# Moving five indirect DMAs in GpSimd's queue of a fused top-k attention and mixture-of-experts kernel

## The chip, the cores and the metric

The kernel runs on one core of one Trainium2 chip. The metric is device time in microseconds (us) of one execution, the median of several runs. In the profile PE is TensorE's matmuls, PEld its weight loads, DVE is VectorE, ACT is ScalarE, POOL is GpSimd and SP is SyncE, which only issues DMAs here.

## The reference, cut to what matters

```python
# attention: 8 batches, 8 heads, 576 tokens, head size 64, top_k = 32
scores = scale * np.matmul(q, k.transpose(0, 1, 3, 2))
kth = np.partition(scores, -top_k, axis=-1)[..., -top_k:-top_k + 1]
scores = np.where(scores >= kth, scores, -1000000000.0)
attn = softmax(scores)
x = np.matmul(attn, v)        # then (B,H,S,D) -> (B*S, H*D) = (4608, 512)
# experts: 8 of them, 512 -> 1024 -> 512, one for each token
logits = x @ w_gate
expert_idx = np.argmax(logits, axis=1)
gate_w = softmax(logits)[np.arange(N), expert_idx]
for e in range(E):            # the rows of expert e, no row dropped
    h = np.maximum(x_sorted[lo:hi] @ w1[e], 0.0)
    y_sorted[lo:hi] = h @ w2[e]
out = gate_w[:, None] * y
```

Everything is float32. The 32nd largest score of each row has to be found exactly, and each attention row goes to one expert.

## The kernel before, in words

**Tiling.** A unit is a pair of heads of one batch, so there are 8 x 4 = 32 units. The attention runs in 144 slots, the passes of the loop at L1250 over `work` (18 slots in a batch, 9 for two units; NT is 9 and NC is 4). A slot handles two tiles of 128 query rows by 576 keys.

**One slot.** TensorE computes the scores three slots ahead (L304), ACT copies them to SBUF (L311), and DVE folds each row's 576 scores into pairwise maxima `h` and minima `l` (`fold`, L320 and L321) and once more (`fold_on`, L327, and L335 or, in some slots, two integer operations on GpSimd, L332 and L333). `search` (L358) then finds the top 32 by four rounds of MAX8 and MATCH_REPLACE8 on DVE (L379, L390). The folds of the next slot ride inside the search of this one: with `soon` after its second round, otherwise ahead of its last, and L320 and L321 come behind it. From the 32nd value ACT makes `low` (L401) and, with a steep ReLU, a mask (`depths`, L417). GpSimd subtracts that from the scores (`less`, L426, two operations), ACT takes the exponential (L434), TensorE transposes the weights (L445, L461), and multiplies them with the values (L482).

**GpSimd's queue in a slot** holds, in order: `nbias` (L385, behind the search's first round of maxima; the exponentials need it), sometimes L332 and L333, the two `less` (L426), `doubts` (L407), and then the indirect DMAs that `put_stores` and `scatter` issue. Every fourth or fifth slot is one "with a unit's rows beside it": the search's callback `beside` (L1271) puts the unit's gate logits (L519 to L524) and its rows (`rows`, L533, a 128x640 multiplication into the tile `x`) right behind `nbias`. Before slot 66 (QUIET) these are the slots whose number leaves 3 or 8 on division by 9. Such a slot is called a rows slot below.

**Scatters and stores.** When a batch's four units are through, its rows go to the experts' places in the DRAM tensor `x_rows`, in five indirect DMAs (L601), one in each slot from number 6 of the next batch on (`scatter(1)`). In the first 66 slots these are slots 24 to 28, 42 to 46 and 60 to 64. After a batch's last scatter its full blocks of 128 rows become work: SP loads their weights and rows, TensorE computes them in pieces between the attention's matmuls (L979, L996), ACT scales the result into `y` (L1005), and the indirect DMA of L888 stores it in the output. The block leaves its store in the list `stores`, and `put_stores` issues it at the end of the next slot's GpSimd work, or from within a block (`following`).

**What sets the order.** The program writes out the order of PE, ACT and DVE by hand (`manual_schedule`), and `in_turn` and `add_manual_dep` keep GpSimd's in the order of the program. `k.crowded` is set by every scatter, store and `rows`; a crowded slot is not `soon` and keeps L335 on DVE instead of L332 and L333 on GpSimd. After slot 143, the remaining expert blocks run on TensorE to the end.

Of the kernel before, what the change touches and what calls it, by code (L numbers as in the profile page):

```python
# [44 lines left out]
def kernel(  # L45
# [54 lines left out]
    NC = 4  # L100
# [7 lines left out]
    NT = 2 * NC + 1  # L108
# [25 lines left out]
    k = SimpleNamespace()  # L134
# [172 lines left out]
    def scores(got):  # L307

        s = k.att.tile([P, 2, 2, HF], F32, name="s", bufs=2 if k.exact else 4)
        return s, [  # L310
            lambda m=m, ps=ps: nc.scalar.copy(s[:, m, :, :], ps[:, :, 0:HF]) for m, ps in enumerate(got)  # L311
        ]

    def fold(s, parts=(slice(0, 2),)):

        f = SimpleNamespace()
        f.h = k.att.tile([P, 2, HF], F32, name="h", bufs=1)
        f.l = k.att.tile([P, 2, HF], F32, name="l")
        for m in parts:
            nc.vector.tensor_tensor(f.h[:, m], s[:, m, 0, :], s[:, m, 1, :], op=ALU.max)  # L320
            nc.vector.tensor_tensor(f.l[:, m], s[:, m, 0, :], s[:, m, 1, :], op=ALU.min)  # L321
        return f
# [696 lines left out]
    QUIET = 66  # L1019
# [4 lines left out]
    with fast:  # L1024
# [8 lines left out]
        per_batch = len(work) // B  # L1033
        x_of, lg_of = {}, {}
        waiting, loaded, coming, spare, scatters, stores = [], [], [], [], [], []
        current = None
        left = clock = 0

        def level(b):

            have, sums = left / PIECES, []
            for n, new in enumerate(new_of[b:] + [0], 1):
                sums.append(have / n)
                have += new
            sums[-1] = (have - KEEP / PIECES) / (len(sums) - 1 + (per_batch - FIRST) / per_batch)
            return min(sums)
# [4 lines left out]
        def ahead():  # L1051
            while waiting and len(loaded) < 2:
                expert, piece = waiting.pop(0)
                if isinstance(piece, SimpleNamespace):
                    rows_in = piece
                elif isinstance(piece, list):
                    rows_in = load_half(load_rows(SimpleNamespace(), piece[0]), *piece[1:])
                elif isinstance(piece, tuple):
                    rows_in = load_rows(SimpleNamespace(), *piece, full=True)
                else:  # L1060
                    rows_in = load_rows(SimpleNamespace(), piece)
                loaded.append(load_weights(rows_in, expert))
                loaded[-1].at = clock

        def put_stores():
            while stores:
                k.crowded = True
                stores.pop(0)()

# [30 lines left out]
        def scatter(n):  # L1100
            nonlocal left
            for _ in range(min(n, len(scatters))):
                k.crowded = True
                scatters.pop(0)()
            if not scatters and coming:
                waiting.extend(coming)
                left += len(coming) * PIECES
                coming.clear()
                ahead()
# [99 lines left out]
        def at_place(name):  # L1209
            for end in list(late):  # L1210
                if end[1] == name:
                    end[1] = next(end[0], None)
                    if end[1] is None:
                        late.remove(end)
# [10 lines left out]
        def multiply(i):  # L1225
            tiles = tiles_of(i)
            got_of[i] = products(tiles, i < AHEAD)
            n, tile = tiles[0]
            more = n.b * U + n.u + 2
            if tile == (NC - 1 if n.u % 2 else 2 * NC) and more < len(units):  # L1230
                unit.append(load_unit(*units[more]))

        def loop():
            nonlocal credit, rate, clock
            for i in range(min(AHEAD, len(work))):
                multiply(i)
                s_of[i], steps = scores(got_of.pop(i))
                for step in steps:
                    step()
            multiply(AHEAD)  # L1240
            for step in prepared:
                step()
            for odd in range(2):
                for h in range(2):
                    r = slice(h * D, (h + 1) * D)
                    at = odd * (lw + P) + h * E
                    nc.vector.tensor_copy(turn[r, :, at:at + E], wg[r, odd::2, :])
            f_of[0] = fold(s_of[0], (slice(0, 1), slice(1, 2)))
            fold_on(f_of[0])
            for i, (b, g) in enumerate(work):  # L1250
                tiles = tiles_of(i)
                u, tile = g[0]
                if tile == 0 and u % 2 == 0:
                    open_unit(tiles[0][0])
                if tails(tiles):
                    open_unit(tiles[1][0])

                loose = 0 < i < QUIET
                k.heavy = loose and "rows" in [place for _, place in late]
                soon = loose and (k.heavy or not k.crowded)  # L1260
                then = behind = beside = lambda: None
                if i + 1 < len(work):
                    def behind():
                        f_of[i + 1] = fold(s_of[i + 1])

                    then = lambda: fold_on(f_of[i + 1], soon and not k.heavy)
                    if i:
                        behind()
                        behind = lambda: None
                if k.heavy:  # L1270
                    beside = lambda: at_place("rows")  # L1271
                held = k.heavy and k.crowded
                low, nbias, doubts = search(tiles, s_of[i], f_of.pop(i), then, soon, behind, beside)
                k.crowded, k.heavy = held, False
                at_place("small")
                w_of[i] = depths(s_of[i], low)
                less(s_of.pop(i), w_of[i])
                doubts()
                at_place("pool")
                if not loose:  # L1280
                    at_place("relu")
                    at_place("rows")
                put_stores()
                scatter(1)
                at = i % per_batch
                if at == FIRST and b:
                    rate = level(b) * PIECES / (U * NT)
                credit += rate * len(g)
                room = left
                if b == B - 1 and at >= ARRIVED:  # L1290
                    room -= KEEP
                    credit = room / (len(work) - i)
                share = {0: 0.5, 1: 1.2, 2: 1.6, 3: 0.5, 2 * NC: 1.4}[tile]
                now = max(0, min(int(credit * share + 0.5), room))
                credit -= now
                clock = i
                if i + AHEAD < len(work):
                    s_of[i + AHEAD], steps = scores(got_of.pop(i + AHEAD))
                    for step in steps:
                        step()  # L1300
                if loose:
                    at_place("relu")
                evacuate()
                at_place("turn")
                turns = turning(i - 1) if i else iter(())
                next(turns, None)
                part = min(BETWEEN, now - now // 2)
                rest = pieces(part)
                next(turns, None)
                rest = pieces(now - now // 2 - part + rest)  # L1310
                weights(tiles, w_of[i], nbias)
                next(turns, None)
                evacuate()
                if i + AHEAD + 1 < len(work):
                    multiply(i + AHEAD + 1)
                if tile == NC - 1:
                    end = ending(b, u)
                    late.append([end, next(end)])
                at_place("products")
                at_place("weights")  # L1320
                credit = min(credit + pieces(now // 2 + rest), 6 * rate)

            k.between = True
            for _ in turning(len(work) - 1):
                pieces(1)
            assert len(late) == 1
            clock = None
            for place in late[0][0]:
                if place == "rows":
                    pieces(4)  # L1330
            kept = left - (SURE + HALVES + PLAIN) * PIECES
            assert kept >= 0, kept
            k.apart = True
            pieces(kept)
# [139 lines left out]
```

## Time and profile before

| What | Value |
|---|---|
| Median of 3 runs (lowest to highest) | 1285.07 us (1283.54 to 1285.09) |
| The profiled execution: its own time | 1284.61 us |
| Its span, first to last instruction | 1283.0 us |
| Busy: PE, PEld | 1176.1 us, 823.6 us |
| Busy: DVE, ACT, POOL | 1058.8 us, 933.3 us, 732.0 us |
| L601, the scatter, on POOL | 40 times, 1065 ns mean |
| L888, the store, on POOL | 37 times, 1052 ns mean (and 4 of 908 ns) |
| L533, `rows`, on POOL | 32 times, 1411 ns mean, 1253 ns at least |
| L320 and L321, the folds on DVE | 145 times each, 770 and 788 ns mean |
| Granted TensorE clock | 0.967 of full speed |

A timeline gives, for each instruction, its start in us from the span's start, its duration in us, the engine, the line, the operation, what it writes and reads, how many were merged, and in brackets the idle time ahead of it with what ended that. An instruction that another engine holds up after it was started shows this as a longer duration, not as idle time.

### The profile page before, as it was taken

How to read it: one execution, taken by the hardware profiler on the slowest of the kernel's cores; microseconds unless marked ns; L12 is line 12 of the kernel's file. 1: busy time of each engine (PE TensorE's matmuls, PEld its weight loads, DVE VectorE, ACT ScalarE, POOL GpSimd, SP SyncE). 2: the span in 40 equal slices, each digit the busy share in tenths (PEclk: the TensorE clock that was granted, in tenths of full speed). 3: DMA queues.
4: the chain of work that ended last, by engine and by line, in shares of the span. 5: the costliest groups of instructions: out<-in, count | busy, mean ns of one | idle time of the engine just before them, and what ended most of it. 6: DMA issues, size and time to landing. Idle time of an engine off the chain costs nothing. (4 is left out here: it accounts for less than half of the span.)

```text
span 1283.0 us, 24461 instructions
## 1 busy us (share of the span) xinstructions
PE 1176.1 (92%) x7574; PEld 823.6 (64%) x7574; DVE 1058.8 (83%) x4608; ACT 933.3 (73%) x2136; POOL 732.0 (57%) x884
## 2 busy tenths in 40 slices
PE   6767767898899999999999999999999999999998
PEld 3444444665566566667666666666666667789975
DVE  8999999999999999999999999999999965000000
ACT  4888887988799888888788888888888872112121
POOL 4777777786678665658555855676557743101010
PEclk9888788999899999999999999999999999999999
DMA  5001113741474147533946464547555548996582
GB/s 153 31 30 31 31 39 126 263 157 39 146 251 162 39 150 283 182 135 98 332 142 218 163 224 153 189 146 264 178 178 202 172 149 285 353 358 235 215 301 83
DMA packets 98701, 220.81 MB, mean 172 GB/s; under 512 B 5309, under 2 KB 26301, under 8 KB 98560
## 3 DMA queue, kind: packets, MB, share of 16 engines
q1 hardware_dynamic: 91360, 198.87, 44.5%
q0 software_dynamic: 6384, 19.97, 4.2%
q8 instruction: 61, 1.00, 0.3%
q14 instruction: 80, 0.66, 0.2%
q10 hardware_dynamic: 816, 0.31, 0.1%
HBM read 195.75 MB, written 24.04 MB: 171 GB/s over the span
## 5 line engine op out<-in xcount | busy, mean ns | idle before, releaser
L426 POOL TENSOR_TENSOR w<-s,w 128x576 f32<-128x576 f32 x288 | 409.2, 1441 | 317.5 <-ACT w L417 317.4
L979 PE MATMUL ph<-xTs,w 128*128 128x128 f32 x2112 | 263.0, 278 | 2.6 <-ACT xTs L870 2.6
L979 PEld LDWEIGHTS ph<-xTs,w 128*128 128x128 f32 x2112 | 251.3, 194 | 21.1 <-issue 17.6
L996 PE MATMUL py<-w,hT 128*128 128x512 f32 x528 | 248.7, 600 | 1.9 <-ACT hT L984 1.6
L434 ACT ACTIVATE w<-w,nbias 128x576 f32<-128x576 f32 x288 | 223.0, 785 | 2.3 <-POOL w L426 1.4
L445 PE MATMUL wTm<-turn,w 128*128 128x128 f32 x1152 | 173.9, 291 | 52.7 <-ACT oT L484 29.1
L417 ACT ACTIVATE w<-s,low 128x576 f32<-128x576 f32 x288 | 207.7, 768 | 4.7
L304 PE MATMUL sc<-qkb 64*128 64x288 f32 (+1 forms) x1280 | 200.7, 465 | 7.8 <-DMA qkb<-in_qk_dram 4.0
L445 PEld LDWEIGHTS wTm<-turn,w 128*128 128x128 f32 x1152 | 135.1, 148 | 111.6 <-ACT oT L484 35.5
L311 ACT COPY s<-sc 128x576 f32<-128x576 f32 x288 | 168.0, 634 | 11.9 <-PE sc L304 11.8
L379 DVE MAX8 tops<-scr 128x8 f32<-128x168 f32 x576 | 169.5, 328 | 0.0
L452 ACT COPY wT<-wTm 128x512 f32<-128x512 f32 x256 | 140.7, 596 | 37.8 <-PE wTm L445 37.2
L379 DVE MAX8 tops<-few 128x8 f32<-128x144 f32 (+1 forms) x576 | 154.9, 314 | 0.0
L304 PEld LDWEIGHTS sc<-qkb 64*128 64x128 f32 (+1 forms) x1280 | 107.1, 190 | 71.5 <-issue 35.2
L996 PEld LDWEIGHTS py<-w,hT 128*128 128x128 f32 x528 | 92.0, 191 | 86.5 <-issue 83.0
L482 PE MATMUL po<-wT,vb 128*64 128x288 f32 x1024 | 143.8, 425 | 0.0
L888 POOL DMA_INDIRECT out_dram<-y,xg x37 | 38.9, 1052 | 161.3 <-ACT y L1005 82.0
L356 DVE MAX8 few<-l 128x8 f32<-128x288 f32 x288 | 129.8, 451 | 0.0
L320 DVE TENSOR_TENSOR h<-s 128x576 f32<-128x576 f32 (+1 forms) x145 | 111.7, 770 | 3.9 <-ACT s L311 3.6
L321 DVE TENSOR_TENSOR l<-s 128x576 f32<-128x576 f32 (+1 forms) x145 | 114.3, 788 | 0.0
L482 PEld LDWEIGHTS po<-wT,vb 128*64 128x64 f32 x1024 | 70.1, 141 | 68.9 <-issue 17.4
L356 DVE MAX8 few<-hl 128x8 f32<-128x72 f32 x576 | 102.3, 221 | 0.0
(205 smaller groups left out, 1596.7 us busy)
## 6 DMA issues: line engine op xcount, KB each, us to landing
w<-in_moe_w_dram SPq DMA_DIRECT2D x74, 2048.0 KB, 9.2
qkb<-in_qk_dram SPq DMA_DIRECT2D x31, 608.0 KB, 3.8
vb<-in_v_dram SPq DMA_DIRECT2D x32, 320.0 KB, 3.2
xg<-x_rows SPq DMA_DIRECT2D x37, 257.0 KB, 9.1
x_rows<-blank SPq DMA_DIRECT2D x13, 257.0 KB, 7.9
x_rows<-blank POOLq DMA_DIRECT2D x4, 257.0 KB, 9.8
x_rows<-x,posi POOLq DMA_INDIRECT x40, 3.2
out_dram<-y,xg POOLq DMA_INDIRECT x37, 3.9
```

What stands on the lines that cost most here:

```text
L304: nc.tensor.matmul(ps[rows, j, 0:HF], n.q[d, cols], n.k[d, keys], start=True, stop=True)
L311: lambda m=m, ps=ps: nc.scalar.copy(s[:, m, :, :], ps[:, :, 0:HF]) for m, ps in enumerate(got)
L356: nc.vector.max(out=f.few[:, m, QF + 8 * j:QF + 8 * j + 8], in_=away)
L379: nc.vector.max(out=tops[:, m, r * 8:(r + 1) * 8], in_=src[m])
L417: nc.scalar.activation(w[:, m, :], s[:, m, :, :].rearrange("p j k -> p (j k)"), AF.Relu, scale=-STEEP, bias=low[:, m:m + 1],)
L426: k.last_pool = in_turn(nc.gpsimd.tensor_tensor(w[:, m, :], s[:, m, :, :].rearrange("p j k -> p (j k)"), w[:, m, :], op=ALU.subtract)).ins
L434: nc.scalar.activation(w[:, m, :], w[:, m, :], AF.Exp, scale=scale, bias=nbias[:, m:m + 1], accum_out=n.z[:, c:c + 1])
L445: nc.tensor.transpose(pm[:, c * P:(c + 1) * P], w[:, m, first:first + P], ident)
L452: nc.scalar.copy(wT[:, :, m, q], pm4)
L482: nc.tensor.matmul(po[r, 0:HF], n.v[:, c, r], rhs, start=(c == 0), stop=(c == KC - 1))
L979: nc.tensor.matmul(ph[:, f, :], n.w1[:, 0, dt, fc * P:(fc + 1) * P], n.xT[:, dt, :], start=(dt == 0), stop=(dt == DT - 1),)
L996: nc.tensor.matmul(py, hT[:, f, :], n.w2[:, 0, f, :], start=(f == 0), stop=(f == FT - 1))
```

## The change

A flag `k.spared` is set in each slot below 65 whose follower is a rows slot (the number leaves 2 or NC + 3 = 7 on division by NT = 9). While it is set, `put_stores` does nothing, and the slot's scatter is left for a later slot. The first slot of a batch's scatters (`at == 6`, which is slot 24, 42 and 60 before QUIET) issues two. The lines that compute `at` move up, and the condition `loose` is 0 < i < QUIET.

```diff
@@ -1035,6 +1035,7 @@
         waiting, loaded, coming, spare, scatters, stores = [], [], [], [], [], []
         current = None
         left = clock = 0
+        k.spared = False
...
         def put_stores():
-            while stores:
+            while stores and not k.spared:
                 k.crowded = True
                 stores.pop(0)()
...
                 if not loose:
                     at_place("relu")
                     at_place("rows")
+                at = i % per_batch
+                k.spared = 0 < i + 1 < QUIET and i % NT in (2, NC + 3)
                 put_stores()
-                scatter(1)
-                at = i % per_batch
+                scatter(1 if not loose else 0 if k.spared else 2 if at == 6 else 1)
```

Built, the two kernels have the same instructions in the same order on PE, ACT, DVE and SP. On POOL five indirect DMAs stand elsewhere: the second scatter of three batches goes from slots 25, 43 and 61 to directly behind the first in slots 24, 42 and 60, and two stores go from slots 38 and 56 to behind `doubts` of slots 39 and 57.

## Prediction

> **What bounds the kernel now.** I read the slices of the page first, to see which engine has no room.
>
> ```profile
> PE   6767767898899999999999999999999999999998
> ...
> DVE  8999999999999999999999999999999965000000
> ```
>
> DVE is full in the first 32 of 40 slices, to the end of the attention's searches (1047 us); then TensorE runs alone to the end. In the first third, where the change acts, TensorE still has holes. DVE's waits between 20 and 1047 us come next (line, what it waited for, us in total, times, longest):
>
> ```profile
> DVE rz L511 <- ACT rz L509: 1.6, 1, 1.6
> DVE h L320 <- ACT s L311: 0.3, 1, 0.3
> DVE h L320 <- POOL hl L332: 0.2, 1, 0.2
> ```
>
> So in 1027 us DVE waited 2.1 us by semaphores. Its instructions keep their order, so it can gain only where an instruction gets shorter. Hence the timelines of slot 26, a rows slot with a scatter (slot 25's) in front: first POOL, then DVE.
>
> ```profile
> 192.16 1.03 POOL L601 DMA_INDIRECT x_rows<-x,posi  x1 [0.16 <-issue]
> 193.23 0.25 POOL L385 TENSOR_SCALAR nbias<-tops 128x2 f32<-128x2 f32 x1
> ...
> 193.83 0.27 POOL L524 TENSOR_TENSOR lg<-xl 128x40 f32<-128x40 f32 x1
> 194.05 1.80 POOL L533 TENSOR_TENSOR x<-xl,rz 128x640 f32<-128x640 f32 x1
> ```
>
> ```profile
> 194.01 0.73 DVE L320 TENSOR_TENSOR h<-s 128x576 f32<-128x576 f32 x1
> 194.66 1.81 DVE L321 TENSOR_TENSOR l<-s 128x576 f32<-128x576 f32 x1
> ```
>
> L533 and L320 start together. L533 stretches from its usual 1.26 to 1.80 us, and then L321, usually 0.74, takes 1.81: they run one after the other. Slot 8 is the same kind of slot without a scatter in front, POOL and then DVE:
>
> ```profile
> 67.87 0.91 POOL L407 TENSOR_TENSOR doubt<-few,tops 128x6 f32<-128x6 f32 x1
> 68.74 0.21 POOL L385 TENSOR_SCALAR nbias<-tops 128x2 f32<-128x2 f32 x1
> ...
> 69.54 1.26 POOL L533 TENSOR_TENSOR x<-xl,rz 128x640 f32<-128x640 f32 x1
> ```
>
> ```profile
> 70.76 0.77 DVE L320 TENSOR_TENSOR h<-s 128x576 f32<-128x576 f32 x1
> 71.42 0.78 DVE L321 TENSOR_TENSOR l<-s 128x576 f32<-128x576 f32 x1
> ```
>
> L533 ends at 70.80 as L320 begins, and neither fold is longer. Last, does TensorE follow DVE? In slot 45, behind the rows slot 44, ACT and then PE show (idle time in brackets):
>
> ```profile
> 329.92 0.20 ACT L401 ACTIVATE low<-tops 128x2 f32<-128x2 f32 x1 [2.38 <-DVE tops L379]
> ```
>
> ```profile
> 333.01 1.11 PE L445 MATMUL wTm<-turn,w 128*128 128x128 f32 x4 [3.10 <-ACT oT L484]
> ```
>
> ACT waits 2.38 us for DVE's search, and TensorE 3.10 us for ACT. Slot 63 shows 2.39 and 2.79 us.
>
> **What the Trainium skill says.** "SBUF — State Buffer", section "Who interferes with whom": a DVE instruction with two SBUF inputs contends with a GpSimd instruction that reads SBUF, and the later one blocks until the first is through. The trace agrees: L320, L321, L327 and L335 (two inputs) get long beside GpSimd's tensor operations, MAX8 beside them doesn't (0.43 to 0.46 us for 288 elements in slots 22 to 28). The same section infers that such a DVE instruction doesn't hinder descriptor generation, which writes. The trace agrees: the scatter at 312.39 took 1.05 us, and L327, which started inside it at 313.07, took its normal 0.44. "DMA: Bandwidth & Descriptors", section "SWDGE vs HWDGE vs iDMA": GpSimd itself computes the descriptors of its DMAs; here a scatter keeps POOL 1065 ns on average.
>
> **The change part by part.**
>
> *The scatter leaves slots 25, 43 and 61.* In slot 26 L407 (191.10, 0.90) ends at 192.00. In slot 8 `nbias` starts as L407 ends and L533 0.80 us later. So L533 would run from about 192.8 to 194.05, and L320, at 194.01, finds it ending. L321 goes from 1.81 back to 0.74: 1.07 us. Slots 44 and 62 show the same picture (L533 at 321.43 and 450.05, L321 with 1.81 each time). All of it lies on DVE, the bound: 3 x 1.07 = 3.2 us gained. POOL's 1.3 us there isn't on the path by itself: `less` waits for ACT's mask anyway.
>
> *It goes behind the first scatter of slots 24, 42 and 60.* POOL then reaches the next `nbias` later. For two indirect DMAs in a row there is a case ahead of slot 45's `nbias`: a store ends at 327.83, the scatter starts at 328.14 and takes 0.96. So `nbias` comes 1.27 us later: at 187.0 instead of 185.76, at 314.75 instead of 313.48, at 443.35 instead of 442.08. Queued behind it are `less` (waiting for ACT's mask until 188.37, 315.58 and 444.19) and, for ACT, the exponentials. In slot 25 it is done by 187.25, ahead of `less`, but touches L320 at 187.11: up to 0.1 us. In slots 43 and 61 it falls within L320 (314.47, 443.08). A scatter's follower in that place is seen in slot 81: `nbias` at 591.12 took 0.94 us and ended 0.09 after L321, which kept 0.74; in slot 77 (561.70) it slipped in between L320 and L321 and took 0.28. In the first way `less` starts some 0.17 us later, and the next slot's L327, which starts as the second `less` ends (318.50 and 318.53), is held up by that. Bounds for each place: nothing, and 0.3 us. I take 0.08 on average, 0.25 in all. No gain is possible here, since this DMA only adds to the queue ahead of `nbias`.
>
> *Two stores leave slots 38 and 56.* There the collision is small now: L522 slips between L320 and L321, and L533 is held up, not DVE.
>
> ```profile
> 284.60 0.77 DVE L320 TENSOR_TENSOR h<-s 128x576 f32<-128x576 f32 x1
> 285.27 0.84 DVE L321 TENSOR_TENSOR l<-s 128x576 f32<-128x576 f32 x1
> ```
>
> Without the store the slot looks like slot 21, which has the same operations and none in front: L533 from 157.40 to 158.66, L320 at 158.27 with 1.00, L321 with 0.75. The sum of both folds goes from 1.61 to 1.75: a loss of 0.14 us, twice, 0.3 us. In slots 39 and 57 the store now stands ahead of the `iota` and `nbias` of the next slot, which `less` follows only at 293.39 after 2.89 us of idling: nothing. If that idle time were gone, it would cost up to its 1.05 us. The store's transfer is later by about 8 us, with no reader.
>
> *Flag and the other slots.* Slots 2, 7, 11, 16, 20, 29, 34, 47 and 52 have nothing to hold back; nothing moves there.
>
> *Sum:* 3.2 - 0.25 - 0.3 = 2.65, say 2.7 us. The profiled execution's 1284.61 (span 1283.0 and 1.6 around it) becomes 1281.9. The median shown is 0.46 above that execution; from 1285.07 the same sum gives **1282.4 us**. A measurement of this kernel can tell about 0.2% (2.6 us) from no change, and the forecast stands just beyond that.
>
> **The rivals.**
>
> *TensorE holds the end.* From 476 to 1047 us PE is busy 558.8 of 571 us. If it didn't come forward with DVE, DVE's head start would go into new collisions, since late masks mean late `less`. For it: nearly no idle time late. Against it: the waits of 2.4 and 3.1 us in slots 45 and 63, longer than the gain of each slot, so that ACT and TensorE move up with DVE before the full stretch begins. Time: 1284.9, no change.
>
> *The wake changes.* From slot 67 on L327 is held up by `less` many times (it takes 1.4 to 1.5 us instead of 0.44 at 506.69, 558.90 and 753.21, for instance). With everything moved alike nothing changes there; but a slightly earlier `less` may spare a collision or two of 1 us each. For it: collisions of all sizes lie there. Against it: the order is the same and both sides of each collision move. Time: 1280.6.
>
> *The second scatter waits for the first to land* (the slower side). The page gives 3.2 us from issue to landing. POOL's queue would stand that long in slots 24, 42 and 60; `nbias` would come 3.2 us later still. In slot 25 it has 1.1 us to spare ahead of `less`, so `less` would be 2.1 us late and hold the next L327 by as much: 3 x 2.1 + 0.3 - 3.2 = 3.4 us slower, 1288.5. It decides from 2.1 us of waiting on (1.1 of slack and 1.0 for the gain). Against it: the scatter behind a store in slot 45 started after 0.3 us. But those two write different tensors.
>
> **How the numbers follow.** The sum as worked out has 0.62: by its bounds (no cost of the second scatters to 0.3 in each place, a residual collision of L533 as in slot 21, 0.24 each) it lies from 1281.4 to 1283.6; 0.38 of it beyond 0.2% and 0.24 within. The wake has 0.14 (faster), TensorE 0.16 (same), the waiting scatter 0.08 (slower). Faster 0.52, same 0.40, slower 0.08. The range from 1280.0 to 1285.4 leaves out the waiting scatter and the outer part of the wake.
>
> **What would show it.** Right: L321 of slots 26, 44 and 62 near 0.75 us, L533 of these near 1.26; L320 of slots 39 and 57 near 1.0; two L601 about 1.3 us apart in slots 24, 42 and 60; the span shorter by the sum already at slot 66. Wrong: a gap above 2 us between the two scatters; L327 of slots 26, 44 and 62 above 0.6; or DVE ahead by 2.7 us at slot 66 and not at slot 143.

## The result and the profile after

| | Changed kernel | Kernel before | Ratio, 95% interval |
|---|---|---|---|
| Median of 22 runs each | 1282.24 us (1279.84 to 1284.01) | 1284.2 us (1281.75 to 1287.5) | 0.9985 (0.9979 to 0.9992) |
| Measured again on another occasion (13 and 29 runs) | 1282.75 us | 1284.76 us | 0.9988 (0.9980 to 0.9997) |
| The profiled execution, time and span | 1281.52 us, 1279.9 us | 1284.61 us, 1283.0 us | |

It is 1.96 us faster by the medians, 1.0 to 2.7 us by the interval. The forecast was 1282.4 us, 2.7 us faster. That the two times lie 0.16 us apart is in part luck: the kernel before came out at 1284.2 us instead of the 1285.07 that the forecast started from, which makes up for a gain that was 0.7 us too large.

In the page's slices nothing has changed its shape; PE and DVE (tenths of each fortieth of the span):

```profile
PE   6767767898989899999999999999999999999998
...
DVE  8999999999999999999999999999999965000000
```

DVE's waits between 20 and 1044 us (line, what it waited for, us in total, times, longest) are as few as before, 2.0 us:

```profile
DVE rz L511 <- ACT rz L509: 1.6, 1, 1.6
DVE h L320 <- ACT s L311: 0.4, 1, 0.4
```

The timeline of slot 26, POOL and then DVE (start, us, engine, line, operation):

```profile
191.41 0.41 POOL L407 TENSOR_TENSOR doubt<-few,tops 128x6 f32<-128x6 f32 x1
191.79 0.42 POOL L385 TENSOR_SCALAR nbias<-tops 128x2 f32<-128x2 f32 x1
...
192.57 0.27 POOL L524 TENSOR_TENSOR lg<-xl 128x40 f32<-128x40 f32 x1
192.79 1.26 POOL L533 TENSOR_TENSOR x<-xl,rz 128x640 f32<-128x640 f32 x1
```

```profile
194.21 0.74 DVE L320 TENSOR_TENSOR h<-s 128x576 f32<-128x576 f32 x1
194.87 0.75 DVE L321 TENSOR_TENSOR l<-s 128x576 f32<-128x576 f32 x1
```

No scatter stands ahead of `nbias`. L533 ends at 194.05, 0.16 us ahead of L320, and L321 takes 0.75 us instead of 1.81. Slots 44 and 62 read the same. In slot 45 ACT and PE still wait, for 1.48 and 2.01 us instead of 2.38 and 3.10, so that both came forward with DVE:

```profile
328.21 0.20 ACT L401 ACTIVATE low<-tops 128x2 f32<-128x2 f32 x1 [1.48 <-DVE tops L379]
```

```profile
331.31 0.66 PE L445 MATMUL wTm<-turn,w 128*128 128x128 f32 x4 [2.01 <-ACT oT L484]
```

In slot 39, where a store is no longer in front, L320 pays as slot 21's does:

```profile
283.71 1.00 DVE L320 TENSOR_TENSOR h<-s 128x576 f32<-128x576 f32 x1
284.64 0.74 DVE L321 TENSOR_TENSOR l<-s 128x576 f32<-128x576 f32 x1
```

Where the time went is best read from stretches, each from a slot's first MAX8 on DVE to the first MAX8 of the slot behind its last. The table gives each profiled execution's stretch less that of the first profile of the kernel before, in us, to about 0.01; the first column is counted from the start of the span. The runs are told below; "before 2" and "before 3" are two more profiles of the kernel before (b1 and b2).

| Slots | 0-25 | 26 | 27-38 | 39 | 44 | 57 | 58-61 | 62 | 67-76 | 77-142 |
|---|---|---|---|---|---|---|---|---|---|---|
| changed | +0.12 | -0.97 | -0.02 | +0.15 | -0.97 | +0.16 | -0.38 | -0.97 | -0.31 | +0.01 |
| changed, again | -0.93 | -0.96 | +0.11 | +0.13 | -0.95 | +0.14 | -0.08 | -0.95 | -0.51 | +0.20 |
| before 2 | -0.69 | -1.03 | +0.31 | -0.02 | +0.02 | -0.01 | -0.10 | +0.02 | -1.56 | +0.15 |
| before 3 | +1.91 | -1.04 | +0.34 | -0.03 | +0.02 | -0.03 | -0.11 | +0.03 | -1.55 | +0.48 |
| scatters only (e1) | +2.44 | -0.97 | +0.08 | -0.03 | -0.96 | -0.02 | -0.38 | -0.96 | -0.33 | +0.54 |
| stores only (e2) | +0.50 | -1.04 | +0.33 | +0.13 | -1.04 | +0.14 | -0.08 | -1.04 | -0.43 | +0.26 |
| two in the rows slot (e3) | +0.39 | -1.04 | +0.09 | -0.03 | -1.04 | -0.01 | -0.37 | -1.04 | -1.94 | +0.53 |
| e3 again (c1) | +1.10 | -1.04 | +0.09 | -0.03 | -1.04 | -0.02 | -0.37 | -1.03 | -1.92 | +0.18 |
| rows behind (e4) | +2.41 | -1.04 | +0.56 | -0.04 | -1.04 | -0.02 | -0.08 | -1.04 | -0.39 | +0.21 |

Of the changed kernel's first profile, slots 26, 44 and 62 hold -2.91 us, 39 and 57 +0.31: -2.6 us in the five places, and -0.5 us elsewhere. The gain lasts to the end: DVE ends its searches 3.1 us earlier, and the span ends 3.1 us earlier too. The rows for the kernel before already show the surprise: without any change, slot 26 can be 1.04 us shorter.

### The profile page after: what moved, and what is told of

It reads as the page before. It is cut to its first block, busy times and chain, and to the rows that moved or that the text cites. A ratio compares the mean times of both kernels' runs of the same rounds, so it can differ in the third digit from the quotient of the medians.

```text
span 1279.9 us, 24461 instructions
## 1 busy us (share of the span) xinstructions
PE 1170.7 (91%) x7574; PEld 819.6 (64%) x7574; DVE 1055.8 (82%) x4608; ACT 932.4 (73%) x2136; POOL 727.7 (57%) x884
## 5 line engine op out<-in xcount | busy, mean ns | idle before, releaser
L320 DVE TENSOR_TENSOR h<-s 128x576 f32<-128x576 f32 (+1 forms) x145 | 112.4, 775 | 3.8 <-ACT s L311 3.8
L321 DVE TENSOR_TENSOR l<-s 128x576 f32<-128x576 f32 (+1 forms) x145 | 110.4, 762 | 0.0
```

## The experiments

The theory on record: DVE is the bound up to the end of the searches, and a fold on DVE (L320, L321) and L533 on GpSimd exclude each other, so that each place is worth what its collision cost (A). Rivals: the scatter itself slows the fold; the gain is a chance change of later collisions (the wake); TensorE holds the end.

**Scatters only (e1).** `put_stores` keeps its old condition.

```diff
-            while stores and not k.spared:
+            while stores:
```

> The scatters move as in the changed kernel, the two stores stay where they were. Theory A (L533 holds DVE's fold up; each place is worth what its collision costs): slots 26, 44 and 62 each shorter by 0.97 us as in the changed kernel, slots 39 and 57 as before (L320 0.77, L321 0.84), so 0.3 us better than the changed kernel: about 2.9 us faster than before, apart from chance in later collisions. Rival W (the gain is mostly a changed wake in later slots, not the three places): no telling sum, the steps by slot differ from place to place. If the stores were of use, it is slower than the changed kernel.

Measured: 1283.16 us against 1284.73, ratio 0.9983 (0.9976 to 0.9990). Slots 26, 44 and 62 gave 0.97, 0.96 and 0.96 us, slots 39 and 57 nothing. Against the first profile, the places are worth what A says; the gain of the whole (1.6 us by the medians, 2.2 by the ratio) is less than their sum (2.9), as with the changed kernel. The profiled execution itself was 2.4 us slower already ahead of slot 24, where no instruction differs.

**Stores only (e2).**

```diff
-                scatter(1 if not loose else 0 if k.spared else 2 if at == 6 else 1)
+                scatter(1)
```

> Only the two stores move, the scatters stay. Theory A: slots 39 and 57 longer by 0.15 us each (L320 1.00, L321 0.75), slots 26, 44 and 62 keep L321 with 1.81; 0.3 us slower than before, which is within 0.2%. Rival S (holding stores back helps, since rows start earlier): slots 39 and 57 shorter and the whole faster.

Measured: 1285.35 us against 1284.73, ratio 1.0005 (0.9997 to 1.0013). Slots 39 and 57 are 0.13 and 0.14 us longer: holding the stores back costs what was worked out. But slots 26, 44 and 62, untouched, are each 1.04 us shorter than in the first profile. Theory A had no place for that. This is their picture in the next run.

**The kernel before, twice more (b1, b2).** No edit.

> The kernel before, unchanged, for a second look at slots 26, 44 and 62. Theory T (L533 and DVE's folds reach the shared read port within some 0.05 us of each other, and which side waits changes from execution to execution): in some of these executions L321 takes 1.81 us, in others L533 takes about 2.5 us and L321 0.74. Rival F (the collision always falls on DVE in this order, and the look at the stores-only kernel was something else): L321 takes 1.81 in all three slots again.

> The kernel before, unchanged, once more. Theory T: either picture, and within one execution the three slots may agree. Rival F: L321 at 1.81 in all three.

The single times were 1282.06 and 1284.66 us. In b1, slot 26 (POOL, then DVE):

```profile
193.37 2.49 POOL L533 TENSOR_TENSOR x<-xl,rz 128x640 f32<-128x640 f32 x1
```

```profile
193.34 0.73 DVE L320 TENSOR_TENSOR h<-s 128x576 f32<-128x576 f32 x1
194.00 0.74 DVE L321 TENSOR_TENSOR l<-s 128x576 f32<-128x576 f32 x1
```

and slot 44 of the same execution:

```profile
320.01 1.81 POOL L533 TENSOR_TENSOR x<-xl,rz 128x640 f32<-128x640 f32 x1
```

```profile
319.96 0.73 DVE L320 TENSOR_TENSOR h<-s 128x576 f32<-128x576 f32 x1
320.62 1.81 DVE L321 TENSOR_TENSOR l<-s 128x576 f32<-128x576 f32 x1
```

L533 starts 0.03 us behind L320 in the one and 0.04 behind in the other. In slot 26 it waits for both folds (2.49 us) and DVE loses nothing; in slot 44 it comes in between them and L321 waits. So theory T holds and rival F falls. Four profiles with the scatters in their old places (the first, b1, b2, e2) show twelve such collisions: DVE lost in seven (3, 2, 2, 0), GpSimd in five. Where GpSimd lost in slot 26, slots 27 to 38 took 0.3 us more, nearly all in slot 27, where a small operation of DVE, L653, took 0.40 us instead of 0.14.

**Rows behind (e4).** Only L533 moves, in slots 26, 44 and 62.

```diff
             logits(n, lg)
-            rows(n, x)
+            if clock is not None and clock + 1 in (26, 44, 62):
+                k.later = lambda: rows(n, x)
+            else:
+                rows(n, x)
...
                 doubts()
+                k.later()
+                k.later = lambda: None
```

> All scatters and stores stay where they were; in slots 26, 44 and 62 alone the rows multiplication L533 moves from behind the logits to behind doubts (L407). Theory A: with L533 out of the way L321 takes 0.74 though the scatter still stands in front: each of the three slots shorter by about 1.07 us, 3.2 us faster than before. Rival R1 (the scatter itself or its transfer slows the fold that follows): L321 stays at 1.81 and nothing is gained. Rival: L533 in its new place collides with L327 of slot 27 (above 0.6 us), and the gain is given back there.

Measured: 1282.9 us against 1284.73, ratio 0.9984 (0.9977 to 0.9990). Slot 26, POOL and then DVE:

```profile
194.58 1.03 POOL L601 DMA_INDIRECT x_rows<-x,posi  x1 [0.16 <-issue]
195.65 0.25 POOL L385 TENSOR_SCALAR nbias<-tops 128x2 f32<-128x2 f32 x1
...
200.60 1.25 POOL L533 TENSOR_TENSOR x<-xl,rz 128x640 f32<-128x640 f32 x1
```

```profile
196.44 0.73 DVE L320 TENSOR_TENSOR h<-s 128x576 f32<-128x576 f32 x1
197.09 0.74 DVE L321 TENSOR_TENSOR l<-s 128x576 f32<-128x576 f32 x1
```

The scatter stands where it stood, L533 is away, and L321 takes 0.74 us in all three slots. So it is L533, not the scatter or its transfer, that DVE collides with; b1 says the same, where the fold of slot 26 isn't slow though the scatter stands in front. By itself this profile can't exclude that GpSimd would have lost anyway; the median of 22 runs, 1.8 us faster and so near the changed kernel's 2.0, speaks for the same cure by another way. It has a price: slots 27 to 38 took 0.56 us more than in the first profile, most of it in slot 27, where L653 took 0.56 us instead of 0.14.

**Two scatters in the rows slot (e3, c1).** The held scatter goes out behind the rows instead of ahead of the slot in front, and the stores stay.

```diff
-            while stores and not k.spared:
+            while stores:
...
-                scatter(1 if not loose else 0 if k.spared else 2 if at == 6 else 1)
+                scatter(1 if not loose else 0 if k.spared else 2 if at == 8 else 1)
```

> The held scatter goes out one slot later, behind the rows slot's own (slots 26, 44, 62 issue two), the stores stay. Theory A: L321 of slots 26, 44 and 62 at 0.74; the 0.1 us that the doubled scatter ahead of slots 25, 43, 61 cost (L327 of the rows slot 0.51 instead of 0.43) is gone too, so each place gives 1.07 instead of 0.97; nbias of slots 27, 45, 63 comes 1.3 us later but ahead of less. In all 3.2 us faster than before. Rival (the second scatter costs wherever it is put): slots 27, 45 or 63 longer by 0.1 us or more and L327 of slots 28, 46, 64 above 0.5.

> The kernel of e3 (two scatters in slots 26, 44 and 62, stores as before) beside the changed kernel on one chip. By the sum of the slots it is 0.6 us faster than the changed kernel (0.1 us less in each of three places and no 0.15 us in slots 39 and 57); the first measurement put it 4 us below before and so 2 us below the changed kernel. Theory A expects 0.3 to 1.2 us between the two; if it is 2 us again, something that the sum of the slots doesn't hold is at work, likely which way later collisions fall.

Measured: 1280.67 us against 1284.73, ratio 0.9965 (0.9954 to 0.9977), and again 1281.26 against 1284.76, 0.9976 (0.9967 to 0.9985), with the changed kernel at 1282.75 on the same chip. Each of the three slots gave 1.04 us instead of 0.97, and slots 39 and 57 stayed short: 0.5 us better than the changed kernel by the places. The difference of the medians there is 1.5 us. The profiles put more than the rest into slots 67 to 76 (-1.94 and -1.92 against -0.31 and -0.51). These are windows of e1, a kernel with the slower stretch, and then of c1 (stretch, its us, each engine's busy us and instructions, granted TensorE clock, DMA share, GB/s):

```profile
490.00:500.00 10.00, 9.36 (x64) 8.56 (x65) 10.00 (x47) 6.17 (x16) 4.88 (x8) 0.83 1.01 373
```

```profile
490.00:500.00 10.00, 10.00 (x85) 8.52 (x86) 10.00 (x41) 7.60 (x20) 3.54 (x6) 1.00 0.88 335
```

TensorE's clock was granted at 0.83 in the one and at 1.00 in the other. The clock's records show what the mean of 0.83 hides: 3.41 us at half speed. All thirteen profiles sort by this. The six with such a piece between 487 and 496 us (the first of the kernel before, both of the changed kernel, e1, e2, e4) have the long stretch, 73.4 to 73.9 us; the seven with none within slots 67 to 76 (b1, b2, e3, c1, e5, e6, e7) have the short one, 71.9 to 72.4. In the six, the masks that ACT makes in slot 70 come 1.4 to 1.7 us later (counted from the start of slot 69), `less` comes later with them, and DVE's L327 there waits: 1.30 to 1.56 us instead of 0.43 to 0.45. The kernel before shows the short stretch in b1 and b2 and the long one in its first profile, so the kernel alone doesn't decide it. Why both e3 profiles have the short one and both of the changed kernel the long one isn't settled: chance is possible with so few. This kernel is the fastest measured here.

**The changed kernel again (c2).** No edit.

> The changed kernel, on the same chip as the kernel of e3. Theory T: L321 of slots 26, 44 and 62 near 0.75 us in this profile too, since L533 is now 1.2 us ahead of the folds and no tie is left; 1.5 to 2.5 us faster than before.

Measured: 1282.75 us against 1284.76, ratio 0.9988 (0.9980 to 0.9997). L321 of the three slots took 0.742, 0.743 and 0.746 us: no tie is left.

**The stall put back (e5).** The changed kernel with a MAX8 more.

```diff
                     def behind():
                         f_of[i + 1] = fold(s_of[i + 1])
+                        if i + 1 in (27, 45, 63):
+                            flat = s_of[i + 1][:, :, :, :].rearrange("p m j k -> p (m j k)")
+                            spare8 = doubt[:, B * U - 1, :, :].rearrange("p t l -> p (t l)")[:, 0:8]
+                            nc.vector.max(out=spare8, in_=flat[:, 0:870])
```

> The changed kernel with one more DVE instruction behind L321 of slots 26, 44 and 62, a MAX8 over 870 elements of the scores (some 1.07 us by the slope from 72 to 288 elements; its result is not used). Theory A (DVE is the bound up to slot 143, and its head start goes to the end one to one): slots 26, 44 and 62 last 1.07 us longer than in the changed kernel, and the whole is 3.2 us slower than it, about 1 us slower than before. Rival P (TensorE holds the end): the whole is within 1 us of the changed kernel.

Measured: 1285.45 us against 1284.01, ratio 1.0011 (1.0003 to 1.0019): 1.4 us slower than before, where the changed kernel is 2.0 us faster by the medians of both occasions (1.9 and 1.5 by the ratios). The instruction took 1048 ns each time. It stands one fold earlier than the expectation said, at the end of the stretches of slots 25, 43 and 61, and made them 0.97, 0.96 and 0.96 us longer than in the changed kernel, 2.9 us in all, of which slots 26, 44 and 62 gave back about 0.25; the times differ by 3.4 us by the medians (3.3 and 3.0 by the ratios). So DVE time spent ahead of slot 66 goes to the end about one to one, within what these medians tell, and rival P falls.

**Rows later (e6).** The kernel before, with two iotas ahead of L533 in slots 26, 44 and 62.

```diff
         k.crowded = True
+        if not k.exact and k.held_up():
+            spare5 = doubt[:, B * U - 1, :, :].rearrange("p t l -> p (t l)")[:, 0:5].bitcast(I32)
+            for _ in range(2):
+                in_turn(nc.gpsimd.iota(spare5, pattern=[[P, KC]], base=0, channel_multiplier=1))
```

> The kernel before with two iotas (0.13 us each, into values that are overwritten later) ahead of L533 in slots 26, 44 and 62, so that L533 starts about 0.25 us behind L320 instead of 0.04 us. All scatters and stores stay. Theory T: L320 is then clearly first; L533 waits for both folds in most executions (2.2 to 2.5 us) and L321 takes 0.74, so about as fast as the changed kernel or 1.5 to 2 us faster than before. Rival: L533 slips in between L320 and L321 every time, L321 takes 1.9 and it is no faster than before or slower.

Measured: 1283.39 us against 1284.01, ratio 0.9999 (0.9991 to 1.0007). My expectation was wrong. In slot 44 (L533 is L537 here; POOL, then DVE):

```profile
321.25 1.52 POOL L537 TENSOR_TENSOR x<-xl,rz 128x640 f32<-128x640 f32 x1
```

```profile
320.92 0.73 DVE L320 TENSOR_TENSOR h<-s 128x576 f32<-128x576 f32 x1
321.57 1.81 DVE L321 TENSOR_TENSOR l<-s 128x576 f32<-128x576 f32 x1
```

With L320 clearly first, by 0.33 us, the multiplication still came in between the folds in two of the three slots (44 and 62) and waited for both in slot 26. So the tie isn't one of arrival ahead of L320: what goes either way is whose turn comes between L320 and L321, when GpSimd already waits. Coming a little later doesn't avoid it; ending before the folds (the changed kernel, e3) or coming behind both (e4) does.

The traces show what goes with the outcome. By their starts in ns, L533 came 29 to 35 ns behind L320 in the five places where it waited for both folds, and 40 to 58 ns behind in the seven where it came in between. In e6 it came 323 ns behind in slot 26, where it waited, and 332 and 333 ns behind in slots 44 and 62, where it came in. In slot 111 it comes 145 to 169 ns behind in every profile but e7's, and comes in every time (in the first profile L320 starts at 812.77, L533 at 812.94, and L321 takes 1.81 us). So what looks like chance may be decided by a few ns of arrival. No run sets these ns, so that isn't shown. Slot 111 also holds a collision of the same size that neither kernel touches.

**Rows first (e7).** As e3, and in `ending` the rows go ahead of the logits, for the whole kernel.

```diff
+            rows(n, x)
             logits(n, lg)
-            rows(n, x)
```

> As e3, and in every rows slot the rows multiplication L533 goes ahead of the unit's logits (L519 to L524), so that it ends some 0.97 us earlier in slots 12, 21, 30, 35, 39, 48, 53 and 57, where it runs into L320 now. Theory A: L320 there takes 0.74 to 0.85 instead of 0.97 to 1.00, with up to 0.1 us given back by L521 or L522 beside L320 or L321: 0.1 to 0.2 us gained in each of some eight slots, 0.8 to 1.6 us faster than e3. Rival (whatever GpSimd does beside the folds costs the same): the sum of L320 and L321 stays 1.72 to 1.75 there, no gain.

Measured: 1286.4 us against 1284.76, ratio 1.0014 (1.0005 to 1.0022). Both theories missed. Slot 21, POOL, and then DVE there and in slot 22:

```profile
159.92 1.45 POOL L522 TENSOR_TENSOR lg<-lg,xl 128x40 f32<-128x40 f32 x1
161.49 1.40 POOL L426 TENSOR_TENSOR w<-s,w 128x576 f32<-128x576 f32 x1
```

```profile
159.83 0.74 DVE L320 TENSOR_TENSOR h<-s 128x576 f32<-128x576 f32 x1
160.49 0.75 DVE L321 TENSOR_TENSOR l<-s 128x576 f32<-128x576 f32 x1
...
163.87 0.71 DVE L327 TENSOR_TENSOR few<-h 128x288 f32<-128x288 f32 x1
```

L320 is down to 0.74, but L522 now waits behind both folds (1.45 instead of 0.27 us), `less` starts late, and L327 of the next slot pays 0.71 instead of 0.48: slot 21 gains 0.25 us and slot 22 loses as much. In slots 39 and 57 L320 takes 1.32 and 1.31 us, and each of these slots is 0.6 us longer than in e3. Behind slot 76, where the edit acts too, slots 77 to 142 became 3.6 us longer.

## Why the prediction was right, and which term was too large

**DVE as the bound, TensorE following: right.** The five places changed DVE's length and the rest followed (e5).

**The scatter leaves slots 25, 43 and 61: the mechanism right, the size too large.** L533 started at 192.79 (forecast 192.8), and L321 fell from 1.81 to 0.75. The term "3 x 1.07 us gained" was read from one execution in which DVE happened to lose all three collisions. With the scatters in their old places it lost seven of twelve. Seven twelfths of 3 x 1.04 is 1.8 us, plus 0.2 for the 0.3 us that slot 27 and its followers lose when GpSimd waits in slot 26 (three of four profiles). Without e2, whose stores stand elsewhere, it is seven of nine and 2.4 us; four profiles don't tell this share better.

**The second scatter: right in its cost.** The pairs start 1.53, 1.35 and 1.35 us apart (forecast 1.3). Here is POOL ahead of slot 44:

```profile
311.66 1.04 POOL L601 DMA_INDIRECT x_rows<-x,posi  x1 [0.17 <-issue]
313.01 0.99 POOL L601 DMA_INDIRECT x_rows<-x,posi  x1 [0.30 <-issue]
314.03 1.20 POOL L385 TENSOR_SCALAR nbias<-tops 128x2 f32<-128x2 f32 x1
315.20 1.40 POOL L426 TENSOR_TENSOR w<-s,w 128x576 f32<-128x576 f32 x1
```

The second waits 0.30 us, not for the first to land: that rival falls. `nbias` waits for both folds in all three places, and L327 of slots 26, 44 and 62 takes 0.50, 0.52 and 0.51 us instead of 0.43. The cost, 0.07 us a place, is what was put down (0.08).

One reading under this term doesn't hold in general. From the scatter at 312.39 the prediction took it that the trace agrees with the inference that it cites, by which a two-input operation of DVE doesn't hinder GpSimd in making the descriptors of a DMA. Up to 1047 us the same profile has five indirect DMAs that start 0.03 to 0.22 us behind an L327, and these take 1.43 to 1.69 us instead of about 1.04; those inside which L327 begins, as at 312.39, take 0.96 to 1.05. One of the five is the scatter of slot 81: it starts at 589.49, behind the L327 of 589.36, and takes 1.59 us. The second scatter of slot 24 in the changed kernel is such a case, with 1.46 us, so that `nbias` there starts at 187.63 and not at 187.0. No run tests the cause.

**The stores: right.** 0.13 to 0.16 us lost twice, forecast 0.14.

**The sum.** 1.8 + 0.2 - 0.2 - 0.3 is 1.5 us, and about 2.1 with seven of nine, against 2.0 us by the medians both times (1.9 and 1.5 by the ratios). In the profiled executions, where the first profile of the kernel before has all three collisions on DVE, the five places give -2.6 us as forecast. The prediction's bounds for the sum don't follow from its terms: from 1285.07 us these give 1282.2 (second scatters free) to 1283.8 (0.3 and 0.24 lost in each place), not 1281.4 to 1283.6.

**The rivals.** "TensorE holds the end" fell with e5. The wake is there in single executions: slots 58 to 61 moved by up to 0.4 us and slots 67 to 76 by up to 1.9, but in 67 to 76 the kernel before moves by 1.6 from one profile to the next, mostly with the piece of half clock told under e3. In the changed kernel's two profiles these stretches together gave 0.7 and 0.6 us; the five places gave 2.6 each time.

## What to carry to other kernels

When two engines take turns at a resource and come to it almost together, one profile shows one outcome: profile the same kernel a few times before a stall is multiplied by the places where it stands. An instruction that is off the critical path is worth moving when its lateness pushes another into the bound engine's two-input operations; it helps if that one then ends before they begin or comes behind both, and not if it merely starts a little later (e6). Check the slot behind as well, since what GpSimd waits for one pair of folds comes back as a late `less` at the next.

## What the runs showed of the hardware that was not expected

- L533 on GpSimd, when it waits behind the fold L320 on DVE, can get its turn between that and the fold L321, or wait for both: it got in at the seven places where it had come 40 to 58 ns behind L320 and at the two where it had come 332 and 333, and waited at the five with 29 to 35 ns and the one with 323. The price on DVE is then 1.07 us (L321 at 1.81 instead of 0.74), else nothing in the folds and 2.2 to 2.5 us for L533 instead of 1.26.
- A single piece of 3.41 us at half of TensorE's clock went with 1.0 to 2.0 us more on DVE, the bound, in slots 67 to 76 (six profiles with it, seven without).
- An indirect DMA that started 0.03 to 0.22 us behind an L327 kept GpSimd for 1.43 to 1.69 us instead of about 1.04 (five in the first profile of the kernel before).
- The time up to slot 24, with the same instructions in all these kernels except e7, was from 0.95 us less to 2.4 us more than in the first profile; this is as large as the effect under study.
